# Loads cut and loads merged: x transposed in three pieces, attention outputs fetched in one load, under an order written out by hand

## The chip, the cores and the metric

The kernel runs on one core of a Trainium2 chip. A core has five engines that run their own instruction lists in order and meet through semaphores: PE (TensorE, matmuls), DVE (VectorE), ACT (ScalarE), POOL (GpSimd) and SP (SyncE, which here only starts transfers). The transfers themselves run on 16 DMA engines. The metric is the device time of one execution in microseconds; the time before is the median of three runs, 242.59 us (242.13 to 242.78). A profile is one more execution, with records of every instruction.

## The reference

The input x has 2048 tokens of 640 numbers. Two branches are mixed by a gate per token, `g * a + (1 - g) * b`.

Branch a is attention with 32 heads of 20 numbers in four segments of 512 tokens, each with causal softmax inside it, and with a memory M, z that collects all earlier segments:

```python
for s in range(N):
    p = softmax(qs @ ks.T * scale + mask); a_dot = p @ vs
    a_mem = (phi(qs) @ M) / (phi(qs) @ z + 1e-6)
    o = g * a_mem + (1.0 - g) * a_dot        # g: sigmoid(beta) of the head
    M = M + phi(ks).T @ vs;  z = z + phi(ks).sum()
a = concat(o) @ wo
```

Branch b multiplies the two-dimensional Fourier transform of x by a weight and transforms back; the kernel does it with matmuls against tables.

## The kernel before

**Stages.** For every segment s, x is loaded transposed (`xT`, 640 rows in five chunks of 128, 512 tokens; two tiles in turn), q, k and v are projected, q and k go through DRAM into padded tiles (`qkp`), PE makes logits, ACT their exponentials (`ex`, three buffers in turn), POOL the causal masks (line 1299), and PE the products with v (`pvf` for segments 0 to 2, `pv` for segment 3). In segments 0 to 2 the unnormalized outputs leave PE transposed, are copied to `ub` and stored to a DRAM scratch `u_scr`, 32 rows per head: 20 rows of output, then the row of denominators. DVE inverts the denominators, and the reciprocals go out to `r_scr`.

**Finishing.** `finish_tile(s, a)` makes 128 tokens of the output. For a = 0 of segments 0 to 2 it fetches the reciprocals of all heads (`ld_r`, tile r) and the outputs (`ld_u`, tile oU): five loads, c = 0 to 4, of 4 rows of each head, 128 partitions of 1 KB each. Each is followed by an operation "normal" (line 1542), `oU[c] = oU[c] * r`, on DVE or POOL. For segments 1 and 2 the memory's share is loaded transposed (`oT`, tile mT) and added (`addmem`, line 1550). Then PE multiplies by `wo`, whose five tiles are loaded with rows in the same order, and adds the other branch (`Fb`). The memory's share is made at line 1172 (segments 1 and 2): DVE reads a PSUM bank as 16 heads x 5 x 4 and writes it in the order that the oU tiles have.

**The Fourier branch's last stage** (`Db`, line 1493) runs beside this: for each n2 of 0 to 15 PE fills two PSUM banks, the first is copied to a staging tile (`eo`, three in turn, index n2 % 3) by ACT or DVE, and DVE makes two sums of the two (`sum_Db`, line 1501), after which the second bank is free. Most matmuls draw from one pool of four PSUM banks ("gen"), the logits from the other four.

**Order.** Every operation is recorded as an `Op` with what it reads and writes. The list `ORDER` gives the sequence: entry v is operation v // 2, and v % 2 picks the engine where there is a choice. `schedule` (line 117) deals this list into one queue per engine and replays it with a cost table (`QUEUE` for transfers: issue cost, work per DMA engine, number of engines) only to choose PSUM banks and semaphores. `emit` (line 258) then writes each engine's instructions in that order, with a `wait_ge` ahead of an instruction for each thing it needs. An engine stands still while it waits; what is behind the waiting instruction waits too. A transfer waits also until all but the latest 1.6 MB of earlier transfers have landed, and for the semaphore (of 56) that it takes.

**SP's order around the change**, from 161 us on: store of ub; oU of segment 0, c = 1; gbc; mT; store of qu; oU c = 0; r; oU c = 3; gcc; store of gT; oU c = 4; reciprocals' store; store of ub; store of qu; oU c = 2; gbc; qkp; r; qkp; oU of segment 1, c = 1 and 2; store of ub; gbc; oU c = 0 and 3; dnc; mT; oU c = 4; wo2; store of gT; qkp; mT; the five oU of segment 2; reciprocals' store. The operations "normal" stand in DVE's list in the order segment 0: c = 1, 3, 2, 0; segment 1: 2, 0, 4, 3; segment 2: 2, 4, 0, 1, 3; and in POOL's list segment 0: 4; segment 1: 1.

Of the kernel before, what the change touches and what calls it, by code (L numbers as in the profile page):

```python
# [445 lines left out]
def dap(ap, off, *dims):  # L446
    return bass.AP(tensor=ap.tensor, offset=ap.offset + off, ap=[list(q) for q in dims])
# [25 lines left out]
class Kern:  # L473
# [83 lines left out]
    def dma(self, dst, src, nbytes, r, w, prio, tr=False, name="", after=(), queue="sp"):  # L557
# [15 lines left out]
        "ld_hm": (600.0, 850.0, 16), "ld_r": (570.0, 700.0, 16), "ld_tt": (530.0, 1650.0, 16), "ld_u": (530.0, 600.0, 16),  # L573
# [1049 lines left out]
```

## Time and profile before

| | |
|---|---|
| median of 3 runs | 242.59 us (242.13 to 242.78) |
| the profiled execution | 240.85 us, its span 238.9 us |
| PE busy | 227.6 us, 95% |
| DVE, ACT, POOL busy | 196.6, 199.5, 166.7 us |
| granted clock of PE, mean | 0.998 |
| transfers of oU | 15 of 128 KB, issued 164.8 to 192.1 us, 2.9 us to landing (median) |
| transposes of x, segments 1 to 3 | 3 of 640 KB, issue 4.18 to 6.09 us each |

Times in the profile are microseconds from the start of the span. In a timeline each line has start, duration, engine, line of the kernel, operation and tiles, and in square brackets how long the engine stood idle before it and what ended the wait. Neighbours of one kind are merged, with their count. Matmuls are pipelined, so that PE busy is not PE at its peak. A DMA's line is its issue on SP, not its transfer.

### The profile page before, as it was taken

What the parts mean: (1) busy time and instruction counts of PE and PEld (TensorE: products, weight loads), DVE (VectorE), ACT (ScalarE), POOL (GpSimd) and SP (SyncE); (2) the same over time, 40 slices, a digit from 0 to 9 for tenths busy, and PEclk for the clock granted to TensorE, in tenths of its full rate; (3) what the DMA queues carried; (4) which work ended last, traced back from release to release, by engine and by line L of the source; (5) the groups of instructions that cost most, each with busy time, mean ns of one, the idle gap of its engine ahead of it and who ended that gap; (6) DMA issues with size and microseconds to landing.
All of it is one profiled execution on the core that took longest, in us unless ns stands there. A gap on an engine that the chain in (4) does not pass through costs nothing.

```text
span 238.9 us, 10255 instructions
## 1 busy us (share of the span) xinstructions
PE 227.6 (95%) x4361; PEld 140.1 (59%) x4361; DVE 196.6 (82%) x481; ACT 199.5 (83%) x241; POOL 166.7 (70%) x297
## 2 busy tenths in 40 slices
PE   7899999999999999999989999999999999899994
PEld 2575566775456566555646655455645466567794
DVE  0579998889899996898999798997988896846563
ACT  2189688898899999999999979999899988797730
POOL 8523268457969956937974999875889868678730
PEclk9999999999999999999999999999999999999999
DMA  7999849996996876483779572364766995872223
GB/s 171 277 366 233 231 125 185 264 207 149 250 227 158 153 210 178 110 241 72 237 213 261 171 226 62 103 157 144 204 205 162 244 215 83 121 107 83 59 86 111
DMA packets 58928, 42.17 MB, mean 177 GB/s; under 512 B 30020, under 2 KB 55172, under 8 KB 58884
## 3 DMA queue, kind: packets, MB, share of 16 engines
q1 hardware_dynamic: 57844, 40.96, 69.9%
q8 instruction: 34, 0.56, 1.0%
q10 hardware_dynamic: 1040, 0.57, 0.8%
q14 instruction: 10, 0.08, 0.2%
HBM read 23.32 MB, written 12.30 MB: 149 GB/s over the span
## 4 chain that ended last, share of the span: by engine, by line
PE 54%; DVE 19%; ACT 14%; DMA 7%; issue 3%; SPq 1%; DVEq 0%
PE psum L529 48%; ACT ex L1278 9%; PE psum L527 6%; DVE Pt L1455 3%; DMA r_scr<-rc 3%; ACT et L1087 2%; DMA xT<-in_A_x_dram 2%; DMA Wt<-in_B_w_i_dram 2%; DVE xsb L921 2%; DVE xf L916 2%; DVE G L1501 1%; DVE va L1130 1%; DVE q L540 1%; DMA r<-r_scr 1%; DVE oU L1542 1%
## 5 line engine op out<-in xcount | busy, mean ns | idle before, releaser
L1278 ACT ACTIVATE ex<-psum 128x2048 bf16<-128x2048 f32 (+4 forms) x92 | 138.7, 1508 | 12.2 <-PE psum L529 10.1
L1299 POOL TENSOR_SCALAR_AFFINE_SELECT ex<-ex 128x256 bf16<-128x256 bf16 (+2 forms) x224 | 122.0, 567 | 37.2 <-ACT ex L1278 33.7
L529 PE MATMUL psum<-qkp 20*64 20x64 bf16 (+5 forms) x1280 | 32.3, 270 | 2.2 <-ACT ex L1278 2.0
L529 PE MATMUL psum<-xT,wk 128*128 128x256 bf16 (+1 forms) x280 | 33.9, 273 | 0.2
L529 PE MATMUL psum<-xT,wq 128*128 128x512 bf16 (+1 forms) x135 | 30.7, 380 | 0.8 <-DMA xT<-in_A_x_dram 0.8
L529 PE MATMUL psum<-wv,xT 128*32 128x321 bf16 (+3 forms) x400 | 30.0, 301 | 0.3 <-DVE va L1130 0.3
L1455 DVE TENSOR_TENSOR Pt<-psum,Wt 128x642 bf16<-128x642 f32 x32 | 25.6, 822 | 2.2 <-PE psum L529 1.9
L529 PEld LDWEIGHTS psum<-qkp 20*64 20x64 bf16 x1280 | 13.3, 102 | 19.7 <-ACT ex L1278 15.4
L529 PEld LDWEIGHTS psum<-xT,wk 128*128 128x128 bf16 (+1 forms) x280 | 19.9, 97 | 6.5 <-DMA wk<-in_A_wk_dram 0.6
L527 PE MATMUL psum<-wo,oU 128*32 128x320 bf16 x480 | 21.9, 300 | 0.7 <-DVE oU L1550 0.5
L921 POOL TENSOR_TENSOR xsb<-xf 128x320 bf16<-128x320 bf16 (+2 forms) x12 | 9.5, 790 | 16.1 <-DVE xsb L921 12.4
L529 PEld LDWEIGHTS psum<-wv,xT 128*32 128x32 bf16 (+1 forms) x400 | 14.6, 96 | 7.5 <-issue 2.6
L1130 DVE TENSOR_TENSOR va<-psum,ebx 128x320 bf16<-128x320 f32 x32 | 15.2, 484 | 4.4 <-ACT gate L1128 2.1
L529 PE MATMUL psum<-big,Ac 128*128 128x160 bf16 (+2 forms) x96 | 18.1, 258 | 0.4 <-DVE Pt L1455 0.3
L529 PE MATMUL psum<-big,Cp 128*128 128x321 bf16 (+1 forms) x96 | 18.0, 302 | 0.2 <-DVE G L1501 0.2
L529 PE MATMUL psum<-ex,va 128*32 128x64 bf16 (+3 forms) x576 | 17.4, 257 | 0.4 <-DVE mem L1175 0.2
L1501 DVE TENSOR_TENSOR G<-eo,psum 128x320 bf16<-128x320 f32 x32 | 14.7, 483 | 3.6 <-PE psum L529 2.6
L540 DVE CAST ot<-psum 128x320 bf16<-128x320 f32 x21 | 10.1, 491 | 9.1 <-PE psum L527 5.9
L529 PE MATMUL psum<-tt,Yt 128*128 128x256 bf16 (+1 forms) x96 | 16.5, 276 | 0.5 <-DVE Yt L1460 0.2
L529 PEld LDWEIGHTS psum<-ex,va 128*32 128x32 bf16 x576 | 10.8, 96 | 9.6 <-POOL ex L1299 1.3
L1087 ACT ACTIVATE et<-qu 128x512 bf16<-128x512 bf16 x25 | 15.6, 631 | 0.2
L527 PEld LDWEIGHTS psum<-wo,oU 128*32 128x32 bf16 x480 | 11.9, 96 | 5.4 <-issue 1.4
(99 smaller groups left out, 392.7 us busy)
## 6 DMA issues: line engine op xcount, KB each, us to landing
qkp<-qk_scr SPq DMA_DIRECT2D x28, 160.0 KB
tt<-tab_tt SPq DMA_DIRECT2D x8, 512.0 KB, 4.5
qk_scr<-qu SPq DMA_DIRECT2D x12, 256.0 KB, 3.1
u_scr<-ub SPq DMA_DIRECT2D x12, 256.0 KB, 3.7
xsb<-in_A_x_dram SPq DMA_DIRECT2D x8, 320.0 KB, 6.5
oU<-u_scr SPq DMA_DIRECT2D x15, 128.0 KB, 2.9
out_dram<-ot SPq DMA_DIRECT2D x12, 160.0 KB
Wt<-in_B_w_r_dram SPq DMA_DIRECT2D x16, 80.2 KB, 2.6
```

Of the source, the lines that this page charges most:

```text
L527: h = e.matmul(dst, wt, r_, start=st, stop=sp_, **{**kw, "tile_position": (0, q), "skip_group_check": True})
L529: h = e.matmul(o_, l_, r_, start=st, stop=sp_, **kw)
L540: alts["dve"] = (lambda e: e.tensor_copy(dst(), src()), 67 + 1.04 * n, 68.0)
L916: self.either(lambda e, r=r, op=op: e.tensor_tensor(xf.ap(r * 642, [321, 2], [1, 320]), xs.ap(o, [D, 2], [1, 320]), xs.ap(o + 320, [D, 2], ...
L921: self.either(lambda e, dst=dst, src=src, d0=d0, n=n, op=op: e.tensor_tensor(xs.ap(o + dst, [D, 2], [1, n]), xf.ap(src + d0, [321, 2], [1, ...
L1087: self.one("act", lambda e: e.activation(et.ap(0, [1, L]), qsl(), ACT.Exp), L, [qb], [b("et", pi_)], late, fix=95, name="phi_exp")
L1130: self.one("dve", lambda e: e.tensor_tensor(va.ap(i * H * VW + h0 * VW, [VW, nh], [1, DH]), self.ps(bank, 0, [DH, nh], [1, DH]), self.ebx. ...
L1278: self.one("act", lambda e, d=d, q=q: e.activation(self.ex.ap(*d), self.ps(bank, *q), ACT.Exp, scale=SC), n, [bank], [self.exb(s, 2 * pr + ...
L1299: self.one("pool", lambda e: e.affine_select(self.ex.ap(e0 + d0, [1280, 4], [1, n], np_=np_), self.ex.ap(e0 + s0, [1280, 4], [1, n], np_=np_),
L1455: self.one("dve", lambda e, ri=ri, Pt=Pt, Wt=Wt, wo_=wo_, bank=bank: e.tensor_tensor(Pt.ap(ri * 322, [644, 2], [1, KD]), self.ps(bank, 0, ...
L1501: self.one("dve", lambda e, q=q, n2=n2, bank=bank, eo=eo: e.tensor_tensor(self.G.ap(n2 * D + 639 * q, [1 - 2 * q, 320]), eo.ap(q, [1, 320] ...
L1542: self.either(lambda e, c=c: e.tensor_tensor(oT.ap(c * L, [1, L]), oT.ap(c * L, [1, L]), self.r4[s].ap(0, [1, L]), ALU.mult), L, [b("r4", ...
```

## The change

Two kinds of loads are regrouped. The transposed load of x for segments 1 to 3 becomes three loads of 2, 2 and 1 chunks, one behind the other at the old one's place. The five loads of oU become one of 640 KB per segment: each of 128 partitions takes five neighbouring rows of `u_scr` (5 KB) instead of five single rows 4 apart. So that tile c of partition (head, j) now holds row 5j + c and not 4c + j, the loads of wo take their rows in the same order, and line 1172 reads PSUM with steps of 5 and 1 (`[1, 5], [5, 4]` in place of `[4, 5], [1, 4]`). The operations "normal" stay five; each now needs the one load. The planner's cost of `ld_u` is set to (640, 3000, 16) from (530, 600, 16). `ORDER` is renumbered; decoded, the lists of PE, ACT, DVE and POOL are the same, and on SP the merged load of each segment stands where the last of its five stood.

```diff
-            self.dma(lambda c=c: self.wo[c].ap(0, [1, D]), lambda c=c: dap(self.wo_d, 4 * c * D, [DH * D, H], [D, 4], [1, D]),
+            self.dma(lambda c=c: self.wo[c].ap(0, [1, D]), lambda c=c: dap(self.wo_d, c * D, [DH * D, H], [5 * D, 4], [1, D]),
...
         if s > 0:
-            self.xt_load(s, self.texp(s - 1, 0) + 6.0 if s > 1 else self.XT1)
+            for c0, n in ((0, 2), (2, 2), (4, 1)):
+                self.xt_load(s, self.texp(s - 1, 0) + 6.0 + 0.01 * c0 if s > 1 else self.XT1, c0, n)
...
-            fn = lambda e: e.tensor_tensor(self.mem.ap(i * D + 64 * q, [4, 16], [P, 5], [1, 4]), self.ps(bank, 0, [VW, 16], [4, 5], [1, 4]),
+            fn = lambda e: e.tensor_tensor(self.mem.ap(i * D + 64 * q, [4, 16], [P, 5], [1, 4]), self.ps(bank, 0, [VW, 16], [1, 5], [5, 4]),
...
+                home = []
+                for c in range(5):
+                    home += self.after_mid(("oU", c)) if s == 0 else []
+                home = home if s == 0 else [b("phq", t) for t in range(5)] if s == 1 else [b("va", 0, lt) for lt in range(4)]
+                self.Sc.group += 1
+                self.dma(lambda: oT.ap(0, [1, 5 * L]),
+                         lambda: dap(self.ud.ap(), s * 1024 * L, [32 * L, H], [5 * L, 4], [1, 5 * L]),
+                         P * 5 * L * 2, [b("ud", s, i) for i in range(4)], ob[:5], prio - 8.0, name="ld_u", after=home)
                 for c in range(5):
                     self.Sc.group += 1
-                    home = self.after_mid(("oU", c)) if s == 0 else [b("phq", t) for t in range(5)] if s == 1 else [b("va", 0, lt) for lt in range(4)]
-                    self.dma(lambda c=c: oT.ap(c * L, [1, L]), lambda c=c: dap(self.ud.ap(), (s * 1024 + 4 * c) * L, [32 * L, H], [L, 4], [1, L]),
-                             P * L * 2, [b("ud", s, i) for i in range(4)], [ob[c]], prio - 8.0, name="ld_u", after=home)
                     self.either(lambda e, c=c: e.tensor_tensor(oT.ap(c * L, [1, L]), oT.ap(c * L, [1, L]), self.r4[s].ap(0, [1, L]), ALU.mult),
                                 L, [b("r4", s)], [ob[c]], prio - 5.0, name="normal")
```

More of the change, by code (lines that the diff above doesn't have):

```diff
@@ L572 @@
         "ld_fcat": (400.0, 350.0, 16), "ld_g": (500.0, 1900.0, 16), "ld_gc": (580.0, 200.0, 16), "ld_gw": (420.0, 600.0, 16),
-        "ld_hm": (600.0, 850.0, 16), "ld_r": (570.0, 700.0, 16), "ld_tt": (530.0, 1650.0, 16), "ld_u": (530.0, 600.0, 16),
+        "ld_hm": (600.0, 850.0, 16), "ld_r": (570.0, 700.0, 16), "ld_tt": (530.0, 1650.0, 16), "ld_u": (640.0, 3000.0, 16),
         "ld_wka": (520.0, 1100.0, 16), "ld_wkb": (450.0, 1500.0, 16), "ld_wqa": (500.0, 1100.0, 16), "ld_wqb": (500.0, 2200.0, 16),
```

190 rows, old and new, of the table ORDER are left out of this document.

## The prediction

> **What bounds the kernel now.** I read the page, then the waits of every compute engine for transfers, then the timelines of SP, DVE and POOL around the moved loads, then transfer durations and the granted clock. The page's first part has TensorE all but saturated:
>
> ```profile
> PE 227.6 (95%) x4361; PEld 140.1 (59%) x4361; DVE 196.6 (82%) x481; ACT 199.5 (83%) x241; POOL 166.7 (70%) x297
> ```
>
> What delays TensorE delays the end, since from 205.6 to 235.8 us its work stands back to back. The waits for transfers after 14 us, over all compute engines, are these four rows (us in total, times, longest):
>
> ```profile
> DVE xf L916 <- DMA xsb<-in_A_x_dram: 0.2, 1, 0.2
> DVE ot L540 <- DMA out_dram<-ot: 1.3, 2, 0.9
> DVE oU L1542 <- DMA r<-r_scr: 0.6, 1, 0.6
> DVE oU L1550 <- DMA mT<-o_scr: 0.6, 1, 0.6
> ```
>
> So transfers cost next to nothing: every load is early enough. What matters is which of them the change makes late. SP's timeline (start, duration) shows the fifteen loads of oU: five for segment 0 up to 174.19, five for segment 1 up to 186.02, five for segment 2 at 189.52 in a row.
>
> ```profile
> 164.85 0.55 SPq L563 DMA_DIRECT2D oU<-u_scr  x1
> ...
> 172.51 1.13 SPq L563 DMA_DIRECT2D u_scr<-ub  x1
> 173.68 0.48 SPq L563 DMA_DIRECT2D qk_scr<-qu  x1
> 174.19 0.53 SPq L563 DMA_DIRECT2D oU<-u_scr  x1
> ...
> 179.77 1.49 SPq L563 DMA_DIRECT2D oU<-u_scr  x2
> 181.68 0.39 SPq L563 DMA_DIRECT2D u_scr<-ub  x1
> ...
> 184.12 0.51 SPq L563 DMA_DIRECT2D dnc<-u_scr  x1
> 184.68 1.29 SPq L561 DMA_TRANSPOSE mT<-o_scr  x1
> 186.02 0.59 SPq L563 DMA_DIRECT2D oU<-u_scr  x1
> ```
>
> Their readers, the "normal" multiplications of line 1542, on DVE (first and third line) and POOL (second):
>
> ```profile
> 172.69 0.42 DVE L1542 TENSOR_TENSOR oU<-oU,r 128x512 bf16<-128x512 bf16 x1
> 183.19 1.16 POOL L1542 TENSOR_TENSOR oU<-oU,r 128x512 bf16<-128x512 bf16 x1
> 184.25 1.56 DVE L1542 TENSOR_TENSOR oU<-oU,r 128x512 bf16<-128x512 bf16 x3
> ```
>
> By the written order the 172.69 one is segment 0's c=1, the 183.19 one segment 1's c=1, and the third of the three at 184.25 (about 185.4) segment 1's c=2. The first reader runs 1.5 us before the last load of its segment is issued.
>
> **The change part by part.** Decoding the order list before and after shows equal sequences on PE, ACT, DVE and POOL. On SP the three transposes stand in place of the one, and each merged load stands where the *last* of its five stood. That decides the case: a multiplication now needs the whole merged load.
>
> *Transposes of x.* Before, they hold SP 5.41, 6.09 and 4.18 us (15.4, 46.7, 77.9). Segment 0's pieces of the same two sizes took 1.21 and, twice, 1.29 us; three pieces with gaps are 3.87, so SP gains 1.5, 2.2 and 0.3 us. On the path: nothing. At most it could gain the 0.2 us of the only transfer wait between 14 and 200 us; it could lose if pieces in a loaded queue took 2.25 us, the longest issue of a small transpose (pkn, 104.7), 6.8 together, 2.6 more than the shortest now; that is covered by SP's own idle time behind them (1.5 us before 55.6, 2 us before 98), and without this cover would delay qkp loads by as much. I take 0, ends -0.2 and +0.5.
>
> *Strided PSUM read of line 1172* (16 instructions of 0.488). The contiguous copy eo<-psum takes 0.481 and the strided Bt<-psum 0.522: 0 to 0.04 x 16 = 0.65 us, on DVE at 63 to 130 us, where PE leads; a gain is excluded, as the element count stays. I take 0. The five loads of wo keep their size; nobody waits for them: 0. The planner replays its lists with a new cost for ld_u, so PSUM banks may be dealt out otherwise; no row prices that, and it is left inside the ends below.
>
> *Segment 0's load.* Four issues of 0.55 us go from the queue, but its successors are held: u_scr<-ub at 172.51 waits for ACT's copy of ub (ends 172.48), so the merged load can start at 173.5 (if that store issues faster than 1.13) to 174.2. I take 173.9. Nothing of 640 KB in 5 KB rows is in the trace. Nearest rows: 128 KB oU, alone, 2.5 us to landing; 512 KB tt, 4.4 (at 149.7, alone); a loaded 320 KB xsb, 6.5. The line through the first two gives 5.0; larger rows should not be worse, so 4.9; ends 4.4 and 6.6. Landing 178.8 instead of being needed at 172.69: DVE stands 6.1 us. Behind it are the second sum (sum_Db) of n2 = 4, then the sums of n2 = 2 and 3 (173.02 to 175.2), each holding a PSUM bank of a pool of four; the staging copy of n2 = 7 on ACT also needs the eo buffer of n2 = 4 (three in turn). PE can work on to about 174.4, then waits for banks: the first comes at 179.45, when the sum of n2 = 4 has run, the next at 181.0 instead of 174.9, so PE is 6.05 late; 0.2 (PE's wait for ACT at 176.16) and some of DVE's 0.78 idle at 176.47 come back. **+5.5**, ends 4.2 and 7.5.
>
> *The clock.* PE stands nearly idle from 174.4 to 181. Granted clock by window (us, five engines' busy time, clock, DMA), after the last matmul at 235.7:
>
> ```profile
> 236.50:237.00 0.50, 0.00 (x0) 0.00 (x0) 0.00 (x0) 0.00 (x0) 0.00 (x0) 1.00 0.57 167
> 237.50:238.00 0.50, 0.00 (x0) 0.00 (x0) 0.00 (x0) 0.00 (x0) 0.00 (x0) 0.82 0.56 169
> 238.00:238.50 0.50, 0.00 (x0) 0.00 (x0) 0.00 (x0) 0.00 (x0) 0.00 (x0) 0.50 0.01 3
> ```
>
> About 2.1 us after the last matmul it halves. The ten warm-up matmuls of 512 columns at 1.30 take 4.45 us, 0.445 each, where later ones follow each other at 0.215 (three in 0.81): half speed for 4.4 us, so up to 2.2 us lost per restart; 0 if the trickle of matmuls keeps the clock up. I take **+1.7** here, where PE leads after the stall. [...]
>
> *Segment 1's load.* SP's place for it is pinned by work that moves with PE: u_scr<-ub (181.68, behind ACT's ub), its landing (dnc at 184.12), the mT transpose; so again at 186.02 plus the delay so far. The last of the five landed after 4.3 us there instead of 2.5 (queue busy, share 0.88 of 184 to 188); two loads ahead of it are gone, so 4.9 + 0.4: landing 191.3, ends 190.4 and 192.6. POOL stands from 183.19, 8.1 us, DVE from 185.4, 5.9. Behind POOL's multiplication are the masks of the exponentials: four (184.29, 2.57 us) and nine (187.88, 5.15), of which the fourth frees PE's pv at 190.93. New: 191.3 + 1.1 + 2.6 + 4 x 0.57 = 197.3, so PE is 6.4 late there. DVE's stall hides beside it: its backlog frees PE's banks by 192.6 and PE has 2.6 us of work up to the pv. **+6.4**, ends 4.5 and 7.5; clock **+0.8**, half of it hidden by the wait for masks.
>
> *Segment 2's load.* SP issues once instead of for 3.17 us. The reciprocals' store behind it (192.74) took 6.7 us to land, and r's load held DVE 0.6 and PE about 0.9 in 204 to 206. With everything else 13 us late, the queue is empty by then: **-0.9**, ends 0 and -1.2.
>
> Sum: 0 + 5.5 + 1.7 + 6.4 + 0.8 - 0.9 = 13.5. The profiled execution took 240.85 (span 238.9, 1.95 around it), 1.74 under the median of 242.59; so 254.35 in a profile and **256.1** in the metric.
>
> [...]
>
> **The rivals.** *One stall is swallowed*: PE's idle gaps (0.9 us in 172 to 184) and DVE's are larger in truth, or SP reaches segment 1's load early. One stall of 7.2 less 0.9 is left: 248.9. Against it: SP's predecessors wait for PE's products. *Not slower*: SP, freed of 4.1 us of transposes and twelve issues of 0.6, issues segment 0's load before 172.69 - 4.9 = 167.8 and segment 1's before 178.3; then only the 0.9 and the 0.2 remain, 241.5 to 242.6. Against it: the qk_scr store at 167.38 and the ub store at 172.51 both stand ahead and wait for ACT. *Worse*: late masks put ACT's exponentials out of step with PE (three ex buffers), or both loads take 6.6: 260 to 264. *No change made*: excluded, the orders differ on SP.
>
> **How the numbers follow.** Both stalls paid 0.70 (250 to 260: down by the clock's 2.5 and the low ends, 1.3 + 1.9 + 0.3; up by the high ends, 2.0 + 1.1, and the 0.9 not won), one swallowed 0.15 (247 to 250), worse 0.10, not slower 0.05. The range 247 to 261 leaves out some 0.17. This kernel's measurement tells about 0.3% (0.7 us) from no change. Slower 0.95, same 0.02, faster 0.03.
>
> **What would show it.** Right: a wait of DVE for the load of oU of about 6 us near 172.7, one of POOL of about 8 us and one of DVE near 191, PE idle beside both, granted clock below 1 there, r's load no longer waited for, xT issues of about 1.3 us. [...]

## The result and the profile after

The changed kernel takes **257.98 us** (median of 6, 257.06 to 260.01) where the kernel before takes 242.69 in the same session: a ratio of **1.0659**, 95% interval 1.0612 to 1.0706, so 15 to 17 us slower. The forecast was 256.1, within 247 to 261. Ratios here compare undisturbed executions alone, while medians hold all of them; where an experiment was disturbed often, its median lies above its ratio. The profiled execution of the changed kernel took 257.06 (span 255.1), 16.2 more than that of before; 1.0 of it is there ahead of the merged loads. TensorE is 0.3 us behind the kernel before at 14 us, 0.8 to 1.1 from 40 us on and 1.0 at 172. Whether the pieces of x have a part in that is not shown: other profiled executions stand 0.2 to 2.4 us behind there, with x whole or in pieces. In what follows the times of after are therefore 1.0 late.

The page: TensorE has 4.4 us more "busy" for the same 4361 matmuls, and the clock row (40 slices) shows why.

```profile
PE 232.0 (91%) x4361; PEld 141.5 (55%) x4361; DVE 199.0 (78%) x481; ACT 199.9 (78%) x241; POOL 167.0 (65%) x297
...
PEclk9999999999999999999999999999579889999999
```

SP's timeline around the merged loads (start, duration):

```profile
173.51 0.36 SPq L563 DMA_DIRECT2D u_scr<-ub  x1
174.72 0.53 SPq L563 DMA_DIRECT2D oU<-u_scr  x1
191.44 0.39 SPq L563 DMA_DIRECT2D u_scr<-ub  x1
193.59 0.53 SPq L563 DMA_DIRECT2D dnc<-u_scr  x1
194.17 1.29 SPq L561 DMA_TRANSPOSE mT<-o_scr  x1
195.50 0.58 SPq L563 DMA_DIRECT2D oU<-u_scr  x1
197.60 1.29 SPq L561 DMA_TRANSPOSE mT<-o_scr  x1
198.93 0.59 SPq L563 DMA_DIRECT2D oU<-u_scr  x1
```

The page's group of these loads (size, median us from issue to landing):

```profile
oU<-u_scr SPq DMA_DIRECT2D x3, 640.0 KB, 5.2
```

The waits of DVE for transfers after 14 us, then POOL's for oU (total, times, longest):

```profile
DVE oU L1548 <- DMA oU<-u_scr: 12.2, 2, 6.2
DVE ot L540 <- DMA out_dram<-ot: 2.0, 3, 1.1
DVE oU L1556 <- DMA mT<-o_scr: 1.4, 1, 1.4
DVE xf L916 <- DMA xsb<-in_A_x_dram: 0.8, 2, 0.6
...
POOL oU L1548 <- DMA oU<-u_scr: 7.8, 1, 7.8
```

The readers that wait, in the timelines of DVE and POOL (in brackets the idle time ahead and what ended it):

```profile
180.00 0.43 DVE L1548 TENSOR_TENSOR oU<-oU,r 128x512 bf16<-128x512 bf16 x1 [6.22 <-DMA oU<-u_scr]
200.75 0.42 DVE L1548 TENSOR_TENSOR oU<-oU,r 128x512 bf16<-128x512 bf16 x1 [6.02 <-DMA oU<-u_scr]
200.80 1.38 POOL L1548 TENSOR_TENSOR oU<-oU,r 128x512 bf16<-128x512 bf16 x1 [7.83 <-DMA oU<-u_scr]
```

Two stalls of DVE and one of POOL, where before there was none; the wait for r is gone, that for mT has grown. TensorE stands beside both (its timeline):

```profile
175.06 0.31 PE L529 MATMUL psum<-big,Cp 128*128 128x321 bf16 x1
180.88 0.98 PE L529 MATMUL psum<-big,Cp 128*128 128x321 bf16 x3 [5.50 <-DVE G L1502]
182.40 1.79 PE L529 MATMUL psum<-big,Cp 128*128 128x321 bf16 x6 [0.53 <-ACT eo L538]
197.94 0.32 PE L529 MATMUL psum<-G,fbg 128*32 128x320 bf16 x4 [0.80 <-ACT ot L538]
202.43 0.46 PE L529 MATMUL psum<-G,fbg 128*32 128x320 bf16 x4 [4.17 <-DVE G L1502]
207.32 0.25 PE L529 MATMUL psum<-va,ex 128*128 128x21 bf16 x4
```

The line at 180.88 is a Db that waits for the PSUM bank of the second sum behind DVE's stalled multiplication; the line at 202.43 is an Fb that waits for such a bank at the second stall. The line at 207.32 is the pv that the forecast let wait for POOL's masks: it has no idle time ahead of it. Granted clock in short windows (the column after the five engines' busy time):

```profile
178.00:178.50 0.50, 0.00 (x0) 0.00 (x0) 0.00 (x0) 0.00 (x0) 0.00 (x0) 0.93 0.87 354
178.50:179.00 0.50, 0.00 (x0) 0.00 (x0) 0.00 (x0) 0.00 (x0) 0.00 (x0) 0.50 0.87 334
...
188.00:188.50 0.50, 0.50 (x18) 0.20 (x16) 0.28 (x2) 0.39 (x1) 0.50 (x1) 0.50 0.43 150
188.50:189.00 0.50, 0.50 (x20) 0.29 (x5) 0.47 (x3) 0.16 (x1) 0.50 (x1) 0.83 0.11 16
...
202.00:202.50 0.50, 0.07 (x4) 0.08 (x8) 0.50 (x2) 0.00 (x0) 0.50 (x2) 0.82 1.73 185
...
205.50:206.00 0.50, 0.50 (x20) 0.27 (x12) 0.50 (x1) 0.50 (x2) 0.50 (x1) 0.76 0.02 0
```

All windows inside the two stretches read 0.50, those around them 1.00; so a window of 0.93 was at half clock for its last 0.07 us, one of 0.83 for its first 0.17. So the clock was halved from 178.43 to 188.67 (10.2 us) after the first stall, though TensorE worked again from 180.88, and from 202.32 to 205.74 (3.4 us) after the second.

Where the time went, by the delay of one instruction each (pvf before, pvf after, pv before):

```profile
180.06 0.73 PE L529 MATMUL psum<-ex,va 128*32 128x512 bf16 x24 [0.18 <-DVE mem L1175]
```

```profile
189.57 0.73 PE L529 MATMUL psum<-ex,va 128*32 128x512 bf16 x24
```

```profile
190.93 0.25 PE L529 MATMUL psum<-va,ex 128*128 128x21 bf16 x4
```

pvf is 9.5 late, of which 8.5 belong to the first stall; pv (190.93 to 207.32) another 6.9; the output projection (205.63 to 222.08) and the end no more. TensorE's share of these stretches divides the two delays (from the same matmul up to pvf, before and after):

```profile
174.06:180.06 6.00, 5.40 (x94) 2.88 (x86) 5.19 (x18) 5.77 (x6) 5.78 (x13) 1.00 0.75 223
```

```profile
175.06:189.57 14.51, 8.48 (x95) 3.97 (x88) 6.58 (x21) 5.96 (x6) 7.15 (x14) 0.65 0.38 117
```

Of the 8.5 us, 5.4 are more idle time (6.0 instead of 0.6) and 3.1 more busy time for the same matmuls, at half clock. From pvf to pv TensorE is busy for 10.54 of 10.87 us before and for 12.21 of 17.75 after: 5.2 more idle, 1.7 more busy.

### The profile page after: what moved, and what is told of

It reads as the page before. It is cut to its first block, busy times and chain, and to the rows that moved or that the text cites. A ratio compares the mean times of both kernels' runs of the same rounds, so it can differ in the third digit from the quotient of the medians.

```text
span 255.1 us, 10252 instructions
## 1 busy us (share of the span) xinstructions
PE 232.0 (91%) x4361; PEld 141.5 (55%) x4361; DVE 199.0 (78%) x481; ACT 199.9 (78%) x241; POOL 167.0 (65%) x297
## 4 chain that ended last, share of the span: by engine, by line
PE 46%; ACT 15%; DVE 14%; DMA 13%; SPq 9%; issue 2%; DVEq 0%
PE psum L529 39%; ACT ex L1279 10%; PE psum L527 6%; SPq L561 5%; DMA xsb<-in_A_x_dram 4%; DMA oU<-u_scr 4%; SPq L563 3%; DVE Pt L1456 3%; DMA qkp<-qk_scr 2%; ACT et L1088 2%; DMA tt<-tab_tt 2%; DVE oU L1548 1%; DVE G L1502 1%; DVE va L1131 1%; DMA u_scr<-ub 1%
## 5 line engine op out<-in xcount | busy, mean ns | idle before, releaser
L529 PE MATMUL psum<-qkp 20*64 20x64 bf16 (+5 forms) x1280 | 33.0, 275 | 2.2 <-ACT ex L1279 1.8
L529 PE MATMUL psum<-big,Cp 128*128 128x321 bf16 (+1 forms) x96 | 20.6, 332 | 6.2 <-DVE G L1502 5.5
L527 PE MATMUL psum<-wo,oU 128*32 128x320 bf16 x480 | 22.6, 308 | 0.5 <-DVE oU L1556 0.5
L1131 DVE TENSOR_TENSOR va<-psum,ebx 128x320 bf16<-128x320 f32 x32 | 15.2, 484 | 4.1 <-ACT gate L1129 2.1
L1548 DVE TENSOR_TENSOR oU<-oU,r 128x512 bf16<-128x512 bf16 x13 | 8.1, 653 | 12.2 <-DMA oU<-u_scr 12.2
```

Source lines behind the costliest of these rows:

```text
L527: h = e.matmul(dst, wt, r_, start=st, stop=sp_, **{**kw, "tile_position": (0, q), "skip_group_check": True})
L529: h = e.matmul(o_, l_, r_, start=st, stop=sp_, **kw)
L1131: self.one("dve", lambda e: e.tensor_tensor(va.ap(i * H * VW + h0 * VW, [VW, nh], [1, DH]), self.ps(bank, 0, [DH, nh], [1, DH]), self.ebx. ...
L1548: self.either(lambda e, c=c: e.tensor_tensor(oT.ap(c * L, [1, L]), oT.ap(c * L, [1, L]), self.r4[s].ap(0, [1, L]), ALU.mult), L, [b("r4", ...
```

## The experiments

Theory: both stalls come from the place of the merged loads, which is where the last of the five stood, while the first reader stood near the first. Rivals: the pieces of x, the shape of the load itself, the way the planner deals PSUM banks.

**The parts alone.** *Only x in pieces*, oU in five loads of the new rows:

```diff
-            self.xt_load(s, self.texp(s - 1, 0) + 6.0 if s > 1 else self.XT1)
+            for c0, n in ((0, 2), (2, 2), (4, 1)):
+                self.xt_load(s, self.texp(s - 1, 0) + 6.0 + 0.01 * c0 if s > 1 else self.XT1, c0, n)
```

> The kernel before with the transposed loads of x in three pieces alone; oU in five loads again, with the new order of rows. Theory (both late loads of oU carry the whole loss): no change, 242.7 us, within 0.7; SP stands some 2 us longer in the transposes in all, as after the change (6.4, 7.0 and 4.45 us instead of 5.4, 6.1 and 4.2), and nobody waits for it. Rival (the longer transposes make SP late for others: the profile after the change is 1.0 us behind at 172 us): 243.5 to 245.

Measured: 243.09, ratio 1.0022 (0.9988 to 1.0057). No change clear of the noise (at most 1.4 us by the interval); the pieces are not the cause.

*One segment's load merged, x whole*, the others in five loads of the new rows:

```diff
+                if (True, False, False)[s]:       # (False, True, False) and (False, False, True) in the other two
                     self.dma(lambda: oT.ap(0, [1, 5 * L]),
```

> The kernel before with oU of segment 0 alone in one load, in the place of the last of its five. Theory: one wait of DVE of 6.2 us near 173, PE idle 5.5 us, granted clock 0.5 for some 8 us behind it; +8.5, so 251.2. Rival (the idle time alone is lost, the clock is made up for elsewhere): +5.5, 248.2.

> The kernel before with oU of segment 1 alone in one load, in the place of the last of its five. Theory: DVE waits some 6 us and POOL some 7.8 us for it, near 185 to 191; +6.9, so 249.6, and with the run on segment 0 alone it adds up to the whole (15.3). Rival (the second wait costs most because the first has put the engines out of step): +3 to +5, 246 to 248.

> The kernel before with oU of segment 2 alone in one load. Theory as revised from the trace after: 0, 242.7, because what stands ahead of the last multiplications on DVE is as late as r; as predicted: 0.9 faster, 241.8, r no longer waited for. Rival (a 640 KB load in the full queue delays the reciprocals' store behind it as much as five did): r waited for as before, 0.6 us, 242.7.

Measured: segment 0 250.89, ratio 1.035 (1.0278 to 1.0421), +8.5 us; segment 1 249.18, 1.0271 (1.0182 to 1.036), +6.6; segment 2 244.06, 1.0006 (0.9955 to 1.0058), nothing. The parts add to 8.5 + 6.6 + 0.1 = 15.2, and the whole is 242.69 x 0.0659 = 16.0; the intervals of the first two are 6.8 to 10.2 and 4.4 to 8.7, so the sum agrees within them and no closer. Each run waits for the oU of its own segment and no other (waits of DVE with segment 0 merged, then of DVE and POOL with segment 1 merged):

```profile
DVE oU L1551 <- DMA oU<-u_scr: 5.3, 1, 5.3
```

```profile
DVE oU L1551 <- DMA oU<-u_scr: 6.0, 1, 6.0
POOL oU L1551 <- DMA oU<-u_scr: 7.8, 1, 7.8
```

The 8.5 of segment 0 alone are not quite the 8.5 of the first stall above: in this profile DVE waits 5.3 instead of 6.2, pvf is 7.5 us late, and 1.4 more are lost behind 205 us, beside a halved stretch (213.4 to 216.8; the mean clock of 206 to 220 is 0.88) that the changed kernel's profile does not have.

With segment 2 merged, r is no longer waited for, but mT is, 0.9 us instead of 0.6.

**The place.** *Merged loads where the first of the five stood* (SP's list, decoded):

```diff
 store of ub
+oU of segment 0, c = 0 to 4
 gbc
...
 reciprocals' store; store of ub; store of qu
-oU of segment 0, c = 0 to 4
```

and likewise for segments 1 and 2.

> The changed kernel, each merged load of oU in the place of the first of its five on SP instead of the last. Theory (only the place matters): segment 0's load issues at about 164.9 and lands 5.2 us later, at 170.1, before its first reader at 172.7; segment 1's issues at 179.8, lands at 185.0, and POOL waits 1.8 us for it, DVE not at all; 242.7 to 244.5. Rival (a load of 640 KB is itself too slow or crowds out others): above 248.

Measured: 245.88, ratio 1.0109 (1.0061 to 1.0157). DVE waits for no load of oU, POOL for 0.9 us: four fifths of the loss are gone with the place alone. Some 2.6 us stay.

*The same with x whole, and POOL's multiplication of segment 1 moved behind four masks*, so that it can't wait either:

```diff
 POOL, decoded
-normal of segment 1, c = 1
 mask, mask, mask, mask
+normal of segment 1, c = 1
```

> Merged loads of oU in the first places, x transposed in one load as before the change, and POOL's multiplication of segment 1 (c = 1) moved behind the four masks that follow it. Theory: no wait for oU is left; 242.0 to 243.0, the same as before within the measurement. Rival (twelve issues fewer on SP bring qkp, r and the stores forward): 241.5 or less.

Measured: 245.49, ratio 1.0101 (1.0043 to 1.0158). The theory missed: no engine waits for oU any more, and the time is the same. TensorE has a new wait, and the clock falls right behind it (timeline, then windows):

```profile
177.67 1.00 PE L529 MATMUL psum<-big,Cp 128*128 128x321 bf16 x6 [1.71 <-ACT eo L538]
```

```profile
172.00:184.00 12.00, 10.21 (x166) 5.50 (x169) 8.69 (x27) 9.23 (x11) 9.40 (x17) 0.86 0.47 138
...
178.50:179.00 0.50, 0.50 (x19) 0.20 (x18) 0.42 (x1) 0.43 (x1) 0.50 (x2) 1.00 0.00 0
179.00:179.50 0.50, 0.50 (x12) 0.38 (x6) 0.15 (x2) 0.41 (x2) 0.50 (x2) 0.66 0.00 0
...
182.50:183.00 0.50, 0.50 (x20) 0.28 (x5) 0.50 (x3) 0.13 (x1) 0.50 (x1) 0.93 0.33 111
```

Before, the same six matmuls waited 0.17 us for DVE's sum (174.95). The order of PE, ACT and DVE is the same, but the planner, replaying it with the new cost of `ld_u` (640, 3000), deals a Db the PSUM bank that ACT's copy frees, behind an exponential, instead of the one that DVE's sum frees. Execution by execution the clock goes with the time: four have a mean granted clock of 0.992 or 0.993 and take 245.41 to 245.79 us, one has 0.999 and takes 243.85, one 0.972 and 249.39 (3.4 us at half clock take 0.007 off the mean of 244 us). New rival, then: the dealing of banks is worth these 2.6 us.

**The dealing.** *Five loads in before's places, x whole, the dealing changed*: only the planner's cost of a load of oU is raised (`ld_v` in this kernel; the loads take the new rows, as in the run with the pieces alone).

```diff
-        "ld_v": (530.0, 600.0, 16),
+        "ld_v": (530.0, 1600.0, 16),
```

> Five loads of oU per segment in their old places and x whole, as before; only the planner's cost of one such load is raised (1600 instead of 600 behind an issue of 530), so that with an unchanged order of every queue eight users of PSUM (five Db, one memory read, one Fb and a Db behind it, a pv among them) get another bank, the first six as in the changed kernel. Theory (the dealing by itself costs what stayed over when the merged loads went first): 244.3 to 245.5, PE standing 1 to 1.7 us behind ACT's copy eo near 175 to 178 us, mean clock of 172 to 184 near 0.86. Rival (the dealing is worth nothing; the 2.4 us came from the one large load): 242.4 to 243.3, window 172 to 184 as before.

*Merged loads in the first places, the dealing of before*: the planner's cost of `ld_u` left as it was.

```diff
-        "ld_u": (640.0, 3000.0, 16),
+        "ld_u": (530.0, 600.0, 16),
```

> The changed kernel with the merged loads in the first places, as in the run of that name, but with the planner's cost of the load as it was (530 and 600), by which every user of PSUM waits for the same predecessor as in the kernel before. Theory (dealing): the 1.71 us wait of PE for ACT's eo is gone and 242.5 to 243.5 is left, no change. Rival (the one large load costs 2.4 us in some other way): 245 to 246, as with the other dealing.

*The changed kernel, merged loads in the last places, the dealing of before*:

```diff
-        "ld_u": (640.0, 3000.0, 16),
+        "ld_u": (530.0, -8000.0, 16),
```

> The changed kernel, merged loads in the last places, but the planner told that they land at once, so that the banks are dealt as in the kernel before (no user of PSUM has another predecessor). Theory (both stalls come from the late load; the dealing hides behind a DVE that stands 6 us anyway): 257 to 258.5, both waits of DVE near 6 us. Rival (part of the 8.5 us of the first stall is the dealing): 254.5 to 256.5.

Measured: 246.1, ratio 1.0112 (1.0067 to 1.0157), for the dealing alone; 243.28, ratio 1.0048 (1.002 to 1.0075), for the first places with before's dealing; 257.41, ratio 1.0643 (1.0559 to 1.0726), for the changed kernel with it. So a number in the planner's table that moves no instruction costs 2.7 us by itself (242.32 x 0.0112; 1.6 to 3.8 by the interval). With it given back the first places are at 1.0048 instead of 1.0109; these two come from different sessions and their intervals overlap. TensorE's wait and its window are then those of before:

```profile
176.09 1.00 PE L529 MATMUL psum<-big,Cp 128*128 128x321 bf16 x6 [0.17 <-DVE G L1502]
...
172.00:184.00 12.00, 11.15 (x216) 6.16 (x215) 10.27 (x32) 11.44 (x16) 10.38 (x18) 1.00 0.56 171
```

In the changed kernel no difference shows beside the stalls (1.0643 and 1.0659): TensorE waits 5.27 and 4.76 us there, with the dealing of the changed kernel 5.50 + 0.53 and 4.17 + 0.80. Merged loads in good places with good banks are still 0.5% behind five loads, and nothing here beats the kernel before. What the profile shows of this rest is POOL's 0.8 us wait for oU, and that POOL's late multiplication then runs beside DVE's three: they take 2.33 us (185.37) instead of the 1.56 of before, TensorE waits 0.28 us behind DVE's sum (188.95) and goes from 1.1 to 1.9 us behind the kernel before. At 222.31 it loses another 0.79, waiting for ACT's copy of ot; what makes that copy late was not followed up.

**The readers.** *Loads in the last places, their readers moved late* (DVE's and POOL's lists, decoded):

```diff
-segment 0: c = 1, 3 at their old places; segment 1: 2, 0 at theirs; POOL c = 1 ahead of the masks
+segment 0: c = 1, 3 just ahead of 2; segment 1: 2, 0 just ahead of 4; POOL c = 1 behind nine masks
```

> The changed kernel with the loads where the change has them (the last places), and the readers moved instead: segment 0's c = 1 and 3 down beside c = 2 and 0 on DVE, segment 1's c = 2 and 0 down to c = 4 on DVE and c = 1 behind the nine masks on POOL. Theory (what is lost is what stands behind the waiting readers, not the landing time): waits for oU under 1 us in all, 242.7 to 244. Rival (the late landing is itself on the path to the first finished tiles): 248 or more.

Measured: 244.64, ratio 1.011 (1.007 to 1.0149), a little above what was expected. DVE waits for no load of oU, POOL for 0.5 us: most of the stall can be taken away from its other end too. What is left stands in 194 to 206 us, where TensorE now waits 0.59, 0.99 and 0.34 us for DVE, the 0.99 for its additions (line 1556), which stand behind the late readers, ahead of the output projection; the clock is at half there from 200.28 to 203.69 (0.86 is its mean in 194 to 206).

**The clock.** *The changed kernel with 22 matmuls of 384 columns that nobody reads ahead of each stall*:

```diff
+        for n in (22, 22):
+            self.hold_clock(n)
```

> The changed kernel with 22 matmuls of 384 columns that nobody reads on PE at each of the two places where it stands still, into a bank of the logits' pool that is free there. They take 3.6 us at full clock, inside the idle time. Theory (some 4 us of the loss are the halved clock after each stall): granted clock near 1 from 176 to 208 us, both waits for oU as long as before, 253.5 to 254.5. Rival (the clock only shows the stall; DVE, ACT and POOL set the pace of the restart): 257 to 258.

Measured: 255.96, ratio 1.0545 (1.0477 to 1.0612), between the two expectations: 2.0 us less by the medians, 2.8 by the ratios. DVE waits as long as ever, 6.4 and 6.0 us. In its timeline the dummies and then a wait that the changed kernel has not; in its windows the clock stays up through both stalls, but one halved stretch comes later, at 207.0 to 210.5 (pvf is the line at 188.00, pv the one at 204.91):

```profile
178.21 3.75 PE L529 MATMUL psum<-fcat 128*128 128x384 bf16 x22 [1.79 <-ACT ex L1290]
188.00 0.73 PE L529 MATMUL psum<-ex,va 128*32 128x512 bf16 x24 [0.17 <-DVE mem L1187]
204.91 0.26 PE L529 MATMUL psum<-va,ex 128*128 128x21 bf16 x4 [0.67 <-POOL ex L1311]
```

```profile
172.00:184.00 12.00, 9.49 (x110) 5.11 (x108) 5.46 (x14) 6.17 (x7) 6.20 (x13) 1.00 0.40 125
184.00:194.00 10.00, 9.44 (x185) 5.18 (x186) 7.79 (x26) 9.45 (x13) 5.48 (x8) 1.00 0.41 108
194.00:204.00 10.00, 8.74 (x127) 4.28 (x115) 5.04 (x10) 4.43 (x5) 4.96 (x8) 1.00 1.04 260
204.00:208.00 4.00, 3.26 (x86) 2.08 (x85) 3.97 (x5) 2.67 (x5) 3.81 (x7) 0.88 0.01 4
208.00:212.00 4.00, 4.00 (x59) 1.62 (x61) 3.59 (x11) 2.14 (x4) 2.62 (x6) 0.69 0.36 90
```

TensorE waits 0.67 us for a mask at pv: the masks decide there only once the clock is held. This profile also prices the clock. pvf is 7.9 us later than in the kernel before, 2.0 of it there ahead of the stall; so the first stall costs 5.9 us with the clock up, instead of 8.5, though DVE waits as long. pv is another 6.0 late instead of 6.9. These 3.5 us are gained up to pv, and the halved stretch behind it takes 1.3 to 1.4 back. In two of the four executions the mean clock is 1.0; they take 255.80 and 254.97 us. With no halved stretch at all the waits alone still cost 12 to 13 us against the 242.78 of before.

*The clock of the first stall alone*: segment 0's load merged, 14 such matmuls.

```diff
+        for n in (14,):
+            self.hold_clock(n)
```

> Only segment 0's load merged, in the last place (it cost 8.5 us by itself), and ahead of the matmul that then waits, 14 matmuls of 384 columns that nobody reads (some 2.4 us at full clock, in a bank of the logits' pool), so that TensorE doesn't stand idle for 5 us. They compute nothing of the output. Theory (the load makes PE late by 5.5 and the halved clock after it costs the other 3.0): 247.5 to 248.6, granted clock 1.00 in 172 to 194, DVE's wait for the load still 5 to 6 us. Rival (the clock costs the 1.7 of the prediction and the stall itself the 6.8 left): 249.0 to 249.8 at a clock of 1.00.

Measured: 253.22 (249.0 to 254.53), ratio 1.0355 (1.0277 to 1.0433), the same as without them (1.035). The time decides nothing: it spreads wide, and the profiled execution loses 5.4 us behind 198 us, where TensorE stands 1.13 and 1.34 us (at 211 and 218) for nothing that the profile shows and the clock is at half from 212.5 to 222.8. The first stall can be read from the trace all the same. TensorE stands 1.79 us ahead of the dummies, as it did above, and here the clock fell, from 178.4 to 181.8 us; but this stretch lies on the dummies, which nobody reads, and the clock is up again for the work behind them:

```profile
188.26 0.73 PE L529 MATMUL psum<-ex,va 128*32 128x512 bf16 x24 [0.17 <-DVE mem L1184]
```

This pvf is 8.2 us later than in the kernel before, 2.2 of it there ahead of the stall. So 6.0 us are left of the 7.5 with segment 0 alone, although DVE waits as long (5.55 and 5.33) and the slow dummies hold the first Db for 0.9 us (it starts 1.78 us behind DVE's multiplication, 0.88 in the changed kernel). Both runs thus give the clock about 2.6 us of the first stall, a little less than the 3.1 of the windows above.

## Why the prediction was right, point by point

*Which waits.* Right: DVE 6.22 (said 6.1) and 6.02 (5.9), POOL 7.83 (8.1), r no longer waited for, the first load pinned behind the ub store (issued at 174.72, less the 1.0 late start 173.7; said 173.9).

*The load's landing.* 5.2 us where the prediction took 4.9 (the line through its two rows gives 5.0; that larger rows are no slower was the author's estimate). Issued at the first places the three take 4.1 to 4.2 (medians of three runs), at the last places 4.6 to 6.1 in the other runs.

*Segment 0's stall,* +5.5: TensorE stands 5.50 and 0.53, less the 0.6 that it stood there before: 5.4. Right by its rows, with the clock aside; the two runs with dummies give 5.9 and 6.0.

*The clock after it,* +1.7: too small. The prediction allowed up to 2.2 us, from the first matmuls, which follow each other at 0.445 us instead of 0.215 for 4.4 us (the granted clock reads 1.00 there), and took 1.7 of them. No run shows the 1.7: the windows give 3.1, the runs with dummies 2.6. The clock was at half for 10.2 us. It stayed there while TensorE worked with gaps (busy for 2.59 us of 180 to 184) and came back at 188.67, behind work without gaps (busy for all of 184 to 188). TensorE was busy for 2.59 + 4.00 + 0.67 = 7.3 us of the 10.2, so up to 3.6 us of work were lost. Other halved stretches lasted 3.4 us (after the second stall, and 179.16 to 182.57 in the run with 245.49), 6.8 (with segment 1 alone, 191.87 to 198.70) and again 10.2 (with segment 0 alone, 175.89 to 186.13); what sets the length was not shown. It is the length that the prediction missed.

*Segment 1's stall,* +6.4 and +0.8 for the clock: 6.6 to 6.9 measured. The sum is near, but another path decided than the one it was worked out on. DVE was to hide beside POOL's masks: banks free by 192.6, and 2.6 us of work for TensorE up to pv. The banks came when it said (202.43, less the 9.5 by which all was late there, is 192.9), but TensorE, which stood 0.80 and 4.17 for them, then needed 4.9 us up to pv, 3.3 of them at half clock (1.7 lost). The masks were ready just before (POOL's timeline, the last one that pv needs):

```profile
206.01 0.66 POOL L1300 TENSOR_SCALAR_AFFINE_SELECT ex<-ex 128x512 bf16<-128x512 bf16 x1
```

It ends at 206.67, less the 9.5 at 197.2, where the prediction had 197.3. So the path that it priced came out as priced, and the one that decided ended 0.65 us behind it: that the sum is near is the luck of these two lying so close. The masks decide where the clock is held, as the run with the dummies shows. By the windows above the 6.9 are 5.2 of waiting and 1.7 of clock, for which the prediction had 0.8, half of the 1.7 that no run shows at the first stall.

*Segment 2's load,* -0.9: wrong, 0. The 0.6 for r did go, but DVE's next wait, for mT, grew from 0.6 to 1.4 in the changed kernel (0.9 with segment 2 alone). The step named no successor for that stall. In the profile with segment 2 alone TensorE also stands 1.6 us near 209 for nothing that the profile shows; why is open.

*The transposes,* 0: right in sum, wrong in the step. SP was to gain 1.5, 2.2 and 0.3 us; the three pieces hold it longer than the whole did in the profile of before (5.41, 6.09, 4.18):

```profile
15.68 6.41 SPq L561 DMA_TRANSPOSE xT<-in_A_x_dram  x3
47.86 7.02 SPq L561 DMA_TRANSPOSE xT<-in_A_x_dram  x3
79.06 4.45 SPq L561 DMA_TRANSPOSE xT<-in_A_x_dram  x3
```

The second lies 0.2 above the bound that the text gave for slow pieces (6.8), the others keep it, and as it said, SP's slack covers it: the run with the pieces alone shows no change.

*The dealing of banks,* left without a price: it is worth 2.7 us by itself (1.6 to 3.8), about as much as the clock of the first stall, and does not show here beside the stalls.

In sum, 13.5 was forecast and 15.3 measured by the medians (16.0 by the ratio): the clock of the first stall (0.9 to 1.4 more) and the gain that didn't come (0.9) make most of the difference, less the 0.3 to 0.6 by which the second stall was smaller than said. No stall was swallowed, and SP reached neither load early, as the rivals had it. The mechanism was right, except for the path that decides at pv; the mis-sized term is the clock of the first stall.

## What to carry to other kernels

When several small loads become one, ask where the first reader of any part stands, not where the last load stood: an engine that works its list in order passes the lateness on to all that is behind it, here 6.22 us of DVE's wait to PSUM banks and so 5.50 us to TensorE. Price a stall of TensorE as the wait plus half of the work done until the clock is back, here 3.4 to 10.2 us later than it fell: after the first stall it stayed down for 7.8 us after work had restarted. And a planner's cost table is part of the kernel: a new number in it can move a buffer behind another engine without moving one instruction.

## What the runs showed of the hardware that was not expected

A transposing load cut in three gained SP nothing, though pieces of these sizes took 1.21 to 1.29 us each elsewhere: in pieces the first two took 0.9 to 1.0 us longer than whole (6.41 and 7.02 against 5.41 and 6.09). Over all profiles the three took 6.3 to 6.4, 6.5 to 7.1 and 4.0 to 4.5 in pieces and 5.4 to 5.5, 5.1 to 6.8 and 3.5 to 4.4 whole; only the first is clear of the scatter. After an idle time of 1.71 us the clock fell in the run with 245.49: it halved at 179.16, when TensorE had been at work again for 1.5 us, and stayed so for 3.4 us of full work; after 1.79 us of idle it stayed up in one run with dummies and fell in the other. Once down, it stayed at one half through 180 to 184 us with TensorE busy 2.59 of 4 us, and through 184 to 188 with TensorE busy throughout; it came up at 188.67.
